# Thirty contraction rows for every score and maxima product of an attention kernel, with the tiles cleared for it and three exponentials one step later

## The chip, the cores and the metric

The kernel runs on one core of one Trainium2 chip. The metric is the device time of one execution in microseconds (us). The engines are named as the profile names them: PE (TensorE, with PEld for its weight loads), DVE (VectorE), ACT (ScalarE), POOL (GpSimd) and SP (SyncE, which here issues most of the DMAs).

## The reference

Two attentions over the same 2048 x 448 input are computed in float32 and mixed by a gate for each row. A is local: each position looks at eight positions, two apart, behind it. B is full attention with 16 heads of 28 columns.

```python
g = _sigmoid((x * gate_w).sum(-1, keepdims=True))
a = _A_ref(x, A_wqkv, A_wo)     # sliding window of 8, dilation 2, 16 heads of 28
b = _B_ref(x, B_wqkv, B_wo)     # scores = q k^T / sqrt(28), softmax, times v, times wo
return g * a + (1 - g) * b
```

## The kernel before

Every float32 operand of a projection or of the scores is held as a rounded value ("hi") and the rest ("lo"); a product is then three products, hi x hi, hi x lo and lo x hi, summed in PSUM. The order of the instructions on each engine is written out by hand (the framework only adds the waits), so an engine does its work in the order in which the program emits it.

**First stage.** The inputs are loaded and split, and q, k, v of both attentions are projected. `init_kh` writes 1.0 over a whole key tile `KH` (128 x 2048) on POOL: a head's 28 rows are later loaded over it, and the rows above keep the ones. The very first split is a cast on DVE (L443), which gives the first 512 columns of `xh`, the first operand of the first projection. Between the projections PE computes the first maxima products, on half the array (64 rows).

**Main stage.** Units are u = 0 to 15 (four heads by 512 queries each), and each has 16 steps, kt = 0 to 15, over blocks of 128 keys. In one step PE issues, in an order given by the list `WITH`: twelve score products (four heads a = 0 to 3, three terms each: token "a0" is KH x QH, "a1" is KH x QL, "a2" is KL x QH), up to three maxima products `s0` to `s2` (a later unit's queries `QP` times `KH`), and then the product `av` of the step before. Each head has a row group of 32 rows of the array, and products of different row groups run side by side. The term "a0" contracts 30 rows, the 28 of the head and two more, in which `QH` holds the negative maximum of the query (hi and lo) and `KH` holds ones; the other products contract 28 rows. ACT takes the exponential of two heads at a time (`P`, 128 x 1024). DVE reduces the maxima (`s1_max`, L155): first `s0` alone, then `s1` and `s2` in one reduction of 1024 columns. A PSUM tile that DVE or ACT still reads can't be written again, so PE's weight loads wait for them.

**Beside it.** The local attention A runs in eight chunks on POOL, DVE and ACT. A planner (`issue`) takes items from a list per engine, each with a key, a cost and the items it needs; an item that is late moves what needs it. ACT's items are the eight local exponentials (`a_softmax(c, 4)`, L679), issued behind the two exponentials of a step. ACT also copies the sums `osb` of the unit that has ended (`fin_copy`, L905, at the start of step kt = 1) and rounds `onhi`, the scaled output of that unit, 14 steps later (`fin_hi`, L943, at the start of kt = 15; the first unit's in two halves, at the start of kt = 0 and kt = 2 of the third unit).

**The end.** When the units are through, the output projection runs on PE alone (L886).

Of the kernel before, what the change touches and what calls it, by code (L numbers as in the profile page):

```python
# [16 lines left out]
NB, NJ, NG = 4, 16, 4  # L17
W, DIL = 8, 2
HALO = (W - 1) * DIL
SCALE = DH ** -0.5  # L20
NU = NG * NB
NMX = 192
# [3 lines left out]
def gated_mix_kernel(ctx: ExitStack, tc: tile.TileContext, xT, xn, gw, wA, wB, woAB, out):  # L26
# [48 lines left out]

    QP = [[cp.tile([128, 512], F32R, name=f"QP{i}{k}") for k in range(2)] for i in range(2)]

    def init_kh(t):
        nc.gpsimd.memset(t.bitcast(F32), 1.0)

    def pair(name):
        return pp.tile([128, 2, 512], F32, tag="P", name=name)
# [18 lines left out]
            r = D + 112 * g + DH * h  # L105
            dma_r(t[32 * h:32 * h + DH, c], src[r:r + DH, c])

    def load_part(u, name, src):
        g, b = divmod(u, NB)
        t = sp.tile([128, 512], F32R, name=name)  # L110
        for h in range(4):
            r = 112 * g + DH * h
            dma_r(t[32 * h:32 * h + DH, :], src[r:r + DH, 512 * b:512 * b + 512])
        return t
# [1 line left out]
    Qs = {}  # L116

    def load_q(u, low=True):
        Qs[u] = load_part(u, "QH", qk_hi), load_part(u, "QL", qk_lo)
        if low:  # L120
            load_nm(u)

# [18 lines left out]
    def s1_mm(n, bank, half=False):  # L141
        u, i = divmod(n, 64)
        qs, kc, h = i // 16, i // 4 % 4, i % 4
        if u == 0:
            qs, kc = i // 8 % 4, 2 * (i // 32) + i // 4 % 2
        if i == 0 and u + 1 < NU:
            load_qhi(u + 1)
        r = slice(64 * (h // 2), 64 * (h // 2) + 64) if half else slice(32 * h, 32 * h + DH)
        nc.tensor.matmul(bank, qhis[u][h % 2][r, 128 * qs:128 * qs + 128],  # L149
                         KH[u // NB % 3][r, 512 * kc:512 * kc + 512], start=True, stop=True)  # L150

# [54 lines left out]
            nc.sync.dma_start(nm[u].bitcast(F32)[:, 32 * a:32 * a + 32], r[32 * a:32 * a + 32, :])  # L206


    for t in KH:
        init_kh(t)  # L210
    t0 = pair("t0")[:, 0, :]
    nc.vector.memset(t0, 0.0)
    nc.vector.memset(zt, 0.0)
    nc.vector.memset(omt, 0.0)

    zero = nc.const_aps.tensor(0.0, [128, 512], F32).bitcast(F32R)

# [8 lines left out]
    if True:  # L226
# [259 lines left out]
        for n, t in enumerate(tiles[:-1]):  # L486
            wi = t[0]
            for w in loads:
                if loads[w] == n:
                    load_w(w)  # L490
            for w in splits:
                i, k = (n - splits[w][0]) * splits[w][1], splits[w][1]
                if 0 <= i < 4:
                    split_w(w, range(i, i + k))
            if n in (3, 5):
                split_x((n + 1) // 2)
            if n < FULL:
                project(n)
            else:
                project_halves(n, [S1_START <= m < S1_START + 80 for m in (n, n + 1)])  # L500
            if n == 0:
                split_x(1, (3,))
            if t[1] == "qk":
                for m in {0: (), 1: (0, 1)}.get(n, (n,)):
                    qk_tile(m, *tiles[m][2:4])
            elif t[1] == "v":
                add_halves(n, V[:, t[2], :, 0:DH])
            else:
                a_tile(n, t[2], t[3])
            if n == 1:  # L510
                split_x(1, range(3))
            if n == 4:
                for t in QP[1]:
                    nc.scalar.activation(t, t0, AF.Copy)
            while fini and fini[0][0] <= n:
                fini.pop(0)[1]()
            if n == 2:
                load_w(1, (False,))
            if n == 3:
                load_qhi(0)  # L520
            if n in (3, 8):
                load_k(0, KH[0], qk_hi, slice(0, 1024) if n == 3 else slice(1024, S))
            if n == 3:
                load_w(1, (True,))
            if n == 16:
                for i in (1, 2):
                    nc.sync.dma_start(a_scr[i][:, 0:NJ, :].rearrange("c j e -> c (j e)").rearrange(
                        "c (a b) -> c a b", b=NJ), omg[0:8, None, :].to_broadcast([8, 56, NJ]))
            if n == 32:
                nc.gpsimd.memset(V[:, :, :, DH:], 1.0)  # L530
            if n == 22:
                load_k(1, KH[1], qk_hi)
            if n == 62:
                load_k(0, KL[0], qk_lo)
            if parts and parts[0][0] <= n:
                _, u, t = parts.pop(0)
                max_store(u, max_turn(t))
            if finished and n < len(tiles) - 3:
                u = finished.pop(0)
                parts.append((n + 3, u, max_parts(u)))  # L540
            if n == 64:
                gate = []
                for sgn, dst in ((-1.0, g_t), (1.0, omg)):
                    e = sp.tile([128, NJ], F32, name="ez")
                    nc.scalar.activation(e, zt, AF.Exp, scale=sgn)
                    nc.gpsimd.tensor_tensor(out=e, in0=e, in1=V[:, 0, :, DH], op=ALU.add)
                    gate.append((dst, e))
            if n in (66, 68):
                nc.vector.reciprocal(*gate.pop(0))
            if n == 70:  # L550
                r = sp.tile([128, 32], F32, name="omr")
                nc.vector.transpose(r, omt)
                for a in range(4):
                    nc.sync.dma_start(og_scr.rearrange("(j p) -> j p", j=NJ)[:, 32 * a:32 * a + 32],
                                      r[32 * a:32 * a + NJ, :])
            if n == 76:
                load_q(0)
# [51 lines left out]
    def main_tiles():  # L609
        nonlocal mp, pm, maskt, actx, a1, a2, a3  # L610
        hctx.close()
        mp = ctx.enter_context(tc.tile_pool(name="mp", bufs=1))

        KH.append(mp.tile([128, S], F32R, name="KH2"))
        KL.append(mp.tile([128, S], F32R, name="KL1"))
        init_kh(KH[2])
        pm = ctx.enter_context(tc.tile_pool(name="pm", bufs=8))

        maskt = mp.tile([128, W, NJ, 2], F32, name="maskt")
        nc.gpsimd.memset(maskt, 0.0)  # L620
        for st, g, t, src in ((12, 2, KH[2], qk_hi), (30, 1, KL[1], qk_lo), (72, 2, KL[0], qk_lo),
                              (100, 3, KH[0], qk_hi), (136, 3, KL[1], qk_lo)):
            at("end", st, lambda g=g, t=t, src=src: load_k(g, t, src))
        for w in range(1, W):
            nc.gpsimd.memset(maskt[0:1, w, 0:DIL * w, :], -1e9 / SCALE)

        actx = ExitStack()
        a1 = actx.enter_context(tc.tile_pool(name="a1", bufs=1))
        a2 = actx.enter_context(tc.tile_pool(name="a2", bufs=2))
        a3 = actx.enter_context(tc.tile_pool(name="a3", bufs=5))  # L630
        for nme in ("k", "v"):
            for i in range(2):
                t = a1.tile([128, HALO + NJ, 56], F32, name=f"{nme}t{i}")
                kvt[nme, i] = t
# [384 lines left out]
    def scores(u, kt, cur):  # L1019
# [9 lines left out]
        for tok in WITH if k else ALONE:  # L1029
            if tok[0] == "s":  # L1030
                i = int(tok[1])
                if i < k:
                    s1_mm(n + i, bank[tok])
                if i == 0:
                    s1_max(n, 1, T1)
                elif i == 2 and k > 1:
                    s1_max(n + 1, k - 1, other[:, 0:k - 1, :])
                continue
            a, t = tok[0], int(tok[1])
            h = (int(a) + n) % 4  # L1040
            r = slice(32 * h, 32 * h + (DH + 2 if t == 0 else DH))
            nc.tensor.matmul(bank[a], (KH[g % 3], KH[g % 3], KL[g % 2])[t][r, ks], (qh, ql, qh)[t][r, :], start=(t == 0), stop=(t == 2))  # L1042
            if t == 2 and a in "20":
                if len(exps) < 5:
                    probs.append(pair("P"))
                p = probs[len(exps) % 5]
                e = nc.scalar.activation(p, one if a == "2" else mine, AF.Exp, scale=SCALE).ins  # L1047
                for o in exps[-5:-4]:
                    tc.declare_no_dep(e, o, query=mybir.DependencyQuery.ANY_SYNC,
                                      reason="PE has read what it wrote, and this one waits for PE")  # L1050
                for o in maxs[-4:]:
                    tc.declare_no_dep(e, o, reason="PE waited for it and the exponential waits for PE")
                exps.append(e)
                cur[(h + 3) % 4], cur[h] = p[:, 0, :], p[:, 1, :]
                yield len(cur)

    for u in range(NU):
        g, b = divmod(u, NB)
        for kt in range(NJ):
# [29 lines left out]
                at("dve", st + lag, lambda t=t, w=turned: w.update(r=counted(lambda: max_turn(t))))  # L1089
                at("end", st + lag, lambda v=v, w=turned: max_store(v, w["r"]))  # L1090
            issue("dve", st, DLIM)
            issue("act", st, 0)
            run("act", st)
            if prev is not None:
                do_av(prev)
# [46 lines left out]
```

## Time and profile before

| | |
|---|---|
| median of 3 runs | 896.78 us (896.74 to 896.83) |
| the profiled execution | 896.69 us, its span 894.9 us |
| PE, DVE, ACT, POOL busy | 99%, 83%, 72%, 71% of the span |
| granted TensorE clock | 1.00 in every stage |
| first and projection stage | about 0 to 248 us |
| main stage, 256 steps | about 248 to 820 us |
| output projection | about 820 us to the end |

The page of the profile counts an engine as busy while one of its instructions runs. Matmuls overlap, so PE's share says that it is never without work, not that it works at its peak. A row of a timeline gives the start, the duration (of the whole run of instructions, where a count "x2" follows), the engine, the line, the operation with the tiles it writes and reads, and in brackets how long the engine had been idle and what released it. For a matmul the form 30*128 means 30 rows of contraction and 128 columns of weights.

### The profile page before, as it was taken

To read this page: it belongs to the slowest core of one execution; us is meant where nothing else is said; L and a number is where in the kernel's file an instruction comes from. 1 tells how busy PE (TensorE), PEld (TensorE's weight loads), DVE (VectorE), ACT (ScalarE), POOL (GpSimd) and SP (SyncE) were. 2 spreads that over 40 slices of the span, in tenths; PEclk is the share of its full clock that TensorE was granted. 3 is DMA by queue.
4 is the path that set the end of the run, shared out by engine and by line. 5 is a ranking of instruction groups with operands and counts; after the bars stand their busy time and mean duration, and the time that the engine had idled before them with its cause. 6 is when DMAs were issued, how large, how long until landed. Compare 5 with 4: busy or idle time off the path is not lost.

```text
span 894.9 us, 20516 instructions
## 1 busy us (share of the span) xinstructions
PE 890.2 (99%) x8312; PEld 533.4 (60%) x8312; DVE 740.5 (83%) x962; ACT 642.4 (72%) x766; POOL 638.7 (71%) x505
## 2 busy tenths in 40 slices
PE   9999999999999999999999999999999999999998
PEld 7889999999954444444444444444444444434997
DVE  6688999999979999999999999999999999832220
ACT  7456434343378898898988989989888898897220
POOL 1499846464459789998999989999999799701000
PEclk9999999999999999999999999999999999999999
DMA  8886403454372241225225222533121322437781
GB/s 267 277 267 186 151 12 84 135 142 121 103 248 66 89 139 46 67 61 156 71 56 143 86 62 86 128 96 98 45 64 32 89 43 49 104 78 214 192 265 52
DMA packets 114038, 104.51 MB, mean 117 GB/s; under 512 B 75240, under 2 KB 82280, under 8 KB 113160
## 3 DMA queue, kind: packets, MB, share of 16 engines
q1 hardware_dynamic: 113512, 102.42, 40.7%
q8 instruction: 65, 1.06, 0.5%
q10 hardware_dynamic: 432, 0.79, 0.3%
q14 instruction: 29, 0.24, 0.1%
HBM read 62.20 MB, written 40.96 MB: 115 GB/s over the span
## 4 chain that ended last, share of the span: by engine, by line
PE 99%; ACT 0%; issue 0%; ACTq 0%
PE T L1042 31%; PE av L1008 28%; PE r L325 15%; PE r L320 8%; PE T L886 8%; PE r L149 4%; PE T L149 4%; PE r L220 0%; PE av L472 0%; ACT P L1047 0%; ACT res L895 0%; ACT onhi L943 0%; ACT L L679 0%; ACTq L943 0%
## 5 line engine op out<-in xcount | busy, mean ns | idle before, releaser
L1047 ACT ACTIVATE P<-T 128x1024 f32<-128x1024 f32 x512 | 496.8, 1023 | 59.6 <-PE T L1042 57.9
L155 DVE TENSOR_REDUCE MX<-T 128x1 f32<-128x512 f32 x470 | 442.5, 954 | 31.7 <-PE T L149 13.7
L1008 PE MATMUL av<-P,V 128*32 128x512 f32 x2048 | 272.7, 605 | 0.0
L1042 PEld LDWEIGHTS T<-QH,KH 30*128 30x128 f32 x1024 | 92.2, 181 | 229.1 <-ACT P L1047 196.5
L149 PE MATMUL T<-KH,QP 28*128 28x512 f32 x704 | 220.3, 456 | 0.1
L1042 PE MATMUL T<-QH,KH 30*128 30x512 f32 x1024 | 211.7, 489 | 0.2 <-ACT P L1047 0.2
L171 DVE TENSOR_REDUCE MX<-r 128x2 f32<-128x1024 f32 x160 | 192.9, 1221 | 20.1 <-PE r L149 16.3
L1042 PE MATMUL T<-QH,KL 28*128 28x512 f32 x1024 | 185.7, 393 | 0.0
L1042 PE MATMUL T<-QL,KH 28*128 28x512 f32 x1024 | 184.3, 392 | 0.0
L653 POOL TENSOR_TENSOR prod<-qt,kt 128x896 f32<-128x896 f32 x64 | 135.4, 2116 | 6.4 <-DMA kt<-a_scr 6.4
L397 ACT ACTIVATE raw<-r 128x896 f32<-128x896 f32 (+1 forms) x62 | 57.1, 921 | 94.5 <-PE r L325 91.9
L149 PE MATMUL r<-KH,QP 64*128 64x512 f32 x320 | 114.5, 391 | 0.0
L714 POOL TENSOR_TENSOR oat<-oat,prod 128x896 f32<-128x896 f32 x48 | 101.2, 2109 | 2.0
L149 PEld LDWEIGHTS T<-KH,QP 28*128 28x128 f32 x704 | 86.1, 181 | 26.7 <-ACT P L1047 17.7
L325 PE MATMUL r<-wh,xh 64*128 64x448 f32 (+1 forms) x504 | 99.6, 363 | 0.0
L709 POOL TENSOR_TENSOR prod<-vt,L 128x896 f32<-128x896 f32 x56 | 95.3, 1702 | 0.3
L398 POOL TENSOR_TENSOR ast<-raw 128x448 f32<-128x448 f32 x47 | 54.3, 1154 | 56.4 <-ACT raw L397 43.9
L1042 PEld LDWEIGHTS T<-QL,KH 28*128 28x128 f32 x1024 | 94.3, 185 | 0.0
L1042 PEld LDWEIGHTS T<-QH,KL 28*128 28x128 f32 x1024 | 93.3, 183 | 0.2
L1008 PEld LDWEIGHTS av<-P,V 128*32 128x32 f32 x2048 | 40.3, 107 | 77.9 <-issue 65.4
L325 PE MATMUL r<-wl,xh 64*128 64x448 f32 (+1 forms) x441 | 79.0, 365 | 0.0
L325 PEld LDWEIGHTS r<-wh,xh 64*128 64x128 f32 x504 | 77.9, 185 | 0.1
(122 smaller groups left out, 1138.8 us busy)
## 6 DMA issues: line engine op xcount, KB each, us to landing
a_scr<-ast SPq DMA_DIRECT2D x24, 448.0 KB
qk_hi<-qkh SPq DMA_DIRECT2D x24, 256.0 KB
qk_lo<-qkh SPq DMA_DIRECT2D x24, 256.0 KB
rbc<-rs SPq DMA_DIRECT2D x64, 64.0 KB
QP<-qk_hi SPq DMA_DIRECT2D x64, 56.0 KB
KL<-qk_lo SPq DMA_DIRECT2D x16, 224.0 KB
QH<-qk_hi SPq DMA_DIRECT2D x64, 56.0 KB
QL<-qk_lo SPq DMA_DIRECT2D x64, 56.0 KB
```

Source lines behind the costliest of these rows:

```text
L149: nc.tensor.matmul(bank, qhis[u][h % 2][r, 128 * qs:128 * qs + 128], KH[u // NB % 3][r, 512 * kc:512 * kc + 512], start=True, stop=True)
L155: i = nc.vector.tensor_reduce(MX[:, n % NMX:n % NMX + k], bank, axis=X, op=ALU.max)
L171: nc.vector.tensor_reduce(m, PM[k], axis=X, op=ALU.max)
L320: nc.tensor.matmul(bank, ws[c][rows, k, t[4]:t[4] + 128], x, start=first, stop=last)
L325: nc.tensor.matmul(bank[:, 0:cols], x, ws[c][rows, k, 0:cols], start=first, stop=last)
L653: nc.gpsimd.tensor_tensor(out=p, in0=qt[c], in1=kvt["k", c % 2][:, HALO - DIL * w:HALO - DIL * w + NJ, :], op=ALU.mult)
L709: nc.gpsimd.tensor_tensor(out=dst.rearrange("p j (h d) -> p j h d", d=DH), in0=kvt["v", c % 2][:, HALO - DIL * w:HALO - DIL * w + NJ, :].r ...
L714: nc.gpsimd.tensor_tensor(out=ows[c % 2][:, :, 0:56] if w == W - 1 else oat[c], in0=oat[c], in1=oat[c, w], op=ALU.add)
L886: writes(bank, nc.tensor.matmul(bank[:, :D], src, wo[c][k], start=(first and k == ks[0] and i == 0), stop=(last and k == ks[-1] and i == 2)))
L1008: nc.tensor.matmul(av[32 * h:32 * h + 32, :], V[:, kt, 4 * g + h, :], tiles_[h], start=(kt == 0), stop=(kt == NJ - 1), skip_group_check=True)
L1042: nc.tensor.matmul(bank[a], (KH[g % 3], KH[g % 3], KL[g % 2])[t][r, ks], (qh, ql, qh)[t][r, :], start=(t == 0), stop=(t == 2))
L1047: e = nc.scalar.activation(p, one if a == "2" else mine, AF.Exp, scale=SCALE).ins
```

## The change

Every score term and every maxima product of the main stage now contracts 30 rows (`ROWS = DH + 2`). So that the two added rows add nothing, `KL` and `QL` are cleared to zero once: `QL` becomes two fixed tiles, cleared on DVE at the start, and `KL` is cleared by a new POOL memset, `init_kl`. The memset of `KH[1]` is emitted later in the program text, beside that of `KL[0]`; that of `KL[1]` stands behind that of `KH[2]`, where the main stage's tiles are made. In `QP` the added rows already hold zeros. The third edit keeps the planner from issuing a local exponential in steps kt = 14 and kt = 0.

```diff
+ROWS = DH + 2
...
+    QL = [cp.tile([128, 512], F32R, name=f"QL{i}") for i in range(2)]
...
+    def init_kl(t):
+        nc.gpsimd.memset(t.bitcast(F32), 0.0)
...
-        Qs[u] = load_part(u, "QH", qk_hi), load_part(u, "QL", qk_lo)
+        Qs[u] = load_part(u, sp.tile([128, 512], F32R, name="QH"), qk_hi), load_part(u, QL[u % 2], qk_lo)
...
-        r = slice(64 * (h // 2), 64 * (h // 2) + 64) if half else slice(32 * h, 32 * h + DH)
+        r = slice(64 * (h // 2), 64 * (h // 2) + 64) if half else slice(32 * h, 32 * h + ROWS)
...
-    for t in KH:
-        init_kh(t)
+    init_kh(KH[0])
...
+    for t in QL:
+        nc.vector.memset(t.bitcast(F32), 0.0)
...
             if n == 4:
                 for t in QP[1]:
                     nc.scalar.activation(t, t0, AF.Copy)
+                init_kh(KH[1])
+                init_kl(KL[0])
...
         init_kh(KH[2])
+        init_kl(KL[1])
...
-            r = slice(32 * h, 32 * h + (DH + 2 if t == 0 else DH))
+            r = slice(32 * h, 32 * h + ROWS)
...
-            issue("act", st, 0)
+            if kt not in (NJ - 2, 0):
+                issue("act", st, 0)
```

**POOL at the start.** What stands on POOL behind the building of the identity matrix, with its waits; before:

```order
masks.py:199 AFFINE_SELECT ident<-ident 128x128 [waits Pool_49]
L83 MEMSET KH_151 128x2048
L83 MEMSET KH_152 128x2048
L235 TENSOR_TENSOR wl_425<-raw,wh_424 128x384 [waits DMAHW7_49,DMAHW0_49,Activation_49]
L235 TENSOR_TENSOR wl_425<-raw,wh_424 128x384 [waits Activation_49] x2
```

and now:

```order
masks.py:199 AFFINE_SELECT ident<-ident 128x128 [waits Pool_49]
L85 MEMSET KH_151 128x2048
L85 MEMSET KH_152 128x2048
L88 MEMSET KL_153 128x2048
L240 TENSOR_TENSOR wl_430<-raw,wh_429 128x384 [waits DMAHW7_49,DMAHW0_49,Activation_49]
L240 TENSOR_TENSOR wl_430<-raw,wh_429 128x384 [waits Activation_49] x2
```

The memset of `KH[1]` (KH_152) stands where it stood, since POOL has nothing else to do ahead of it, and no wait holds it back; the memset of `KL[0]` (KL_153) follows it directly.

**DVE at the start**, where the first cast waits for its input from DRAM; before:

```order
L212 MEMSET t_161 128x512
L213 MEMSET zt 128x16
L214 MEMSET omt 128x32
L443 CAST xh_181<-V 128x512
L448 TENSOR_TENSOR xl_185<-V,xh_181 128x512
```

and now:

```order
L215 MEMSET t_162 128x512
L216 MEMSET zt 128x16
L217 MEMSET omt 128x32
L219 MEMSET QL_155 128x512
L219 MEMSET QL_156 128x512
L448 CAST xh_184<-V 128x512
```

The two memsets of `QL` stand ahead of the cast.

**ACT around the end of the seventh unit** (two `P` rows are a step; `L` is the local exponential, `onhi` the rounding at kt = 15, `osb` the copy at the next unit's kt = 1); before:

```order
L1047 ACTIVATE P<-T_3241 128x1024
L1047 ACTIVATE P<-T_3237 128x1024
L679 ACTIVATE L<-L 128x256
L943 ACTIVATE onhi<-on 128x512
L1047 ACTIVATE P<-T_3241 128x1024
L1047 ACTIVATE P<-T_3233 128x1024
L1047 ACTIVATE P<-T_3241 128x1024
L1047 ACTIVATE P<-T_3237 128x1024
L905 ACTIVATE osb<-av 128x512
```

and now:

```order
L1055 ACTIVATE P<-T_3245 128x1024
L1055 ACTIVATE P<-T_3241 128x1024
L951 ACTIVATE onhi<-on 128x512
L1055 ACTIVATE P<-T_3245 128x1024
L1055 ACTIVATE P<-T_3237 128x1024
L687 ACTIVATE L<-L 128x256
L1055 ACTIVATE P<-T_3245 128x1024
L1055 ACTIVATE P<-T_3241 128x1024
L913 ACTIVATE osb<-av 128x512
```

The local exponential has moved behind the next step's two exponentials. Three of the eight move so, by one step each: this one, the one at the end of the second unit, which comes to stand directly ahead of the first half of `onhi`, and the one after that, whose chunk has become a step later. With them, items of three chunks on DVE, POOL and SP that need them stand up to a step later. PE's order is unchanged, instruction by instruction.

More of the change, by code (lines that the diff above doesn't have):

```diff
@@ L106, in load_k, with load_part @@
             dma_r(t[32 * h:32 * h + DH, c], src[r:r + DH, c])
-    def load_part(u, name, src):
+    def load_part(u, t, src):
         g, b = divmod(u, NB)
-        t = sp.tile([128, 512], F32R, name=name)
         for h in range(4):
```

## The prediction

> **What bounds the kernel now.** I read the page first: busy shares, then the chain that ended last.
>
> ```profile
> PE 890.2 (99%) x8312; PEld 533.4 (60%) x8312; DVE 740.5 (83%) x962; ACT 642.4 (72%) x766; POOL 638.7 (71%) x505
> PE 99%; ACT 0%; issue 0%; ACTq 0%
> ```
>
> PE is the chain from the first matmul to the last. So whatever delays PE's start is paid in full, and in the main stage a stall shows only as a product that starts later than its row group was free. The second view is the busy time of the main stage.
>
> ```profile
> 255.00:780.00 525.00, 524.82 (x5366) 218.79 (x5365) 494.31 (x698) 467.51 (x523) 479.43 (x334) 1.00 0.33 88
> ```
>
> DVE (third, 494.31) works 94% of these 525 us, ACT (fourth, 467.51) 89%: a gain on PE here can't exceed DVE's idle 30.7 us. The third view is the timeline of one step, about 2.2 us long.
>
> ```profile
> 390.83 1.23 DVE L155 TENSOR_REDUCE MX<-T 128x2 f32<-128x1024 f32 x1
> 391.93 0.18 PEld L1042 LDWEIGHTS T<-QH,KH 30*128 30x128 f32 x2 [0.84 <-ACT P L1047]
> 391.94 0.50 PE L1042 MATMUL T<-QH,KH 30*128 30x512 f32 x2
> 391.94 0.50 PE L149 MATMUL T<-KH,QP 28*128 28x512 f32 x1
> 392.04 0.19 PEld L1042 LDWEIGHTS T<-QL,KH 28*128 28x128 f32 x2
> 392.12 0.18 PEld L1042 LDWEIGHTS T<-QH,KH 30*128 30x128 f32 x2
> 392.12 0.49 PE L1042 MATMUL T<-QH,KH 30*128 30x512 f32 x1
> 392.28 0.40 PE L1042 MATMUL T<-QL,KH 28*128 28x512 f32 x2
> 392.28 0.39 PE L1042 MATMUL T<-QH,KH 30*128 30x512 f32 x1
> ```
>
> The step opens at 391.93. The weights of the second pair of 30-row terms load at 392.12, which is 0.06 after DVE's two-bank reduction ended (390.83 + 1.23 = 392.06). DVE's reduction, not PE, releases them.
>
> **Thirty rows for all products.** Here is what the different row counts cost now, by the groups of instructions.
>
> ```profile
> L1042 PE MATMUL T<-QH,KH 30*128 30x512 f32 x1024 | 211.7, 489 | 0.2 <-ACT P L1047 0.2
> L1042 PE MATMUL T<-QL,KH 28*128 28x512 f32 x1024 | 184.3, 392 | 0.0
> L149 PE MATMUL r<-KH,QP 64*128 64x512 f32 x320 | 114.5, 391 | 0.0
> ```
>
> The 30-row products look 97 ns dearer than the 28-row ones (489 against 392 ns). It isn't the rows: 64 rows take 391. In the step above the 28-row maxima product at 391.94, which also opens its row group, takes 0.50 like the 30-row ones beside it, and the 30-row product at 392.28, whose weights had been loaded ahead, takes 0.39. The 0.1 us is a weight load that nothing covers, and it stays.
>
> Nor does a change of the row count cost anything here. From 30 to 28: the 28-row weights at 392.04 load while the 30-row products of the same row groups run, 0.11 after the first load. From 28 to 30 in one row group: the product at 392.28 follows the maxima product of 391.94 after 0.34, no more than a 28-row product takes behind a 30-row one (391.94 to 392.28, also 0.34). So I take 0 for this part. Its bounds: a gain of the whole apparent 0.1 us on PE's chain in each of some 235 steps (704 maxima products, three to a step), 23 us, which is a rival below; and on the other side 1 ns a product (391 against 392 ns for 64 and 28 rows), under 1 us in all. The DMAs into `QL` and `KL` keep their sizes and their places ahead of their users.
>
> **The memsets at the start.** Each row that decides here:
>
> ```profile
> 1.25 3.54 POOL L83 MEMSET KH<- 128x2048 f32 x2
> 0.91 0.48 DVE L212 MEMSET t<- 128x512 f32 x1 [0.91 <-PEq L1134]
> 1.35 0.07 DVE L213 MEMSET zt<- 128x16 f32 x1
> 4.64 0.43 DVE L443 CAST xh<-V 128x512 fp32r<-128x512 f32 x1 [3.18 <-DMA V<-in_xT]
> 0.77 4.37 PE L220 MATMUL r<-const-float32-0.0 128*128 128x512 f32 x10 [0.77 <-PEq L1134]
> 5.22 0.71 PE L320 MATMUL r<-xh,wh 128*128 128x512 f32 x2
> 6.89 0.63 PE L320 MATMUL r<-xh,wh 128*128 128x512 f32 x2
> 7.36 0.62 PE L320 MATMUL r<-xl,wh 128*128 128x512 f32 x2
> ```
>
> The two `QL` memsets cost DVE 2 x 0.48 = 0.96 us from about 1.5 on, and DVE is idle until 4.64: nothing. POOL's memsets don't hold DVE's back (the one at 1.35 took 0.07 with POOL's first memset running); if they did, the 0.96 would come on top of the wait weighed next.
>
> POOL's order hasn't set its tiles out of DVE's way. Two memsets of 1.80 us each fill 1.25 to 4.79, and the third, of `KL[0]`, now follows at 4.73 (they overlap by 0.06) and ends at 6.53. The cast comes at 4.64, the only DVE instruction of this kind near it. What can happen to such a cast shows elsewhere.
>
> ```profile
> 783.15 1.29 POOL L947 TENSOR_TENSOR onlo<-on,onhi 128x512 fp32r<-128x512 f32 x1 [2.49 <-DVE KH L830]
> 783.29 1.40 DVE L829 CAST KH<-wor 128x448 fp32r<-128x448 f32 x1
> 785.62 0.35 DVE L829 CAST KH<-wor 128x448 fp32r<-128x448 f32 x1
> 817.08 1.29 POOL L947 TENSOR_TENSOR onlo<-on,onhi 128x512 fp32r<-128x512 f32 x1 [8.11 <-DVE onhi L941]
> 817.92 0.73 DVE L862 CAST onhi<-oar 64x512 fp32r<-64x512 f32 x1 [0.92 <-DMA oar<-oa_scr]
> 809.76 0.43 DVE L862 CAST oahi<-oar 128x512 fp32r<-128x512 f32 x1 [7.40 <-DMA oar<-oa_scr]
> ```
>
> A cast that starts under a POOL instruction waits for it: 1.40 and 0.73 instead of 0.35 and 0.43, each ending 0.25 to 0.28 behind POOL. The cast of the start took its plain 0.43, as at 809.76, though the second memset covered its first 0.15; either a memset doesn't hold a cast, or the wait fell into the cast's own start. So the bounds are 0 and a wait for the whole third memset, to 6.53 + 0.28 = 6.81 instead of 5.07: 1.74 us. As the first projection (5.22) needs the cast and PE has no slack from 6.89 on (two matmuls each 0.47), all of it would be paid. I take 0: the cast starts 0.09 ahead of the third memset. But a DMA that lands 0.1 us later turns this round.
>
> [...]
>
> **`KL[1]`.** This memset of 1.80 us stands behind that of `KH[2]` on POOL.
>
> ```profile
> 254.95 0.21 POOL L192 TENSOR_TENSOR nmt<-nmv,nmt 128x16 fp32r<-128x16 f32 x1
> 261.60 2.13 POOL L653 TENSOR_TENSOR prod<-qt,kt 128x896 f32<-128x896 f32 x1 [6.44 <-DMA kt<-a_scr]
> 259.25 0.20 DVE L201 STREAM_TRANSPOSE nms<-nmt 128x32 f32<-128x32 f32 x1
> ```
>
> It moves `nmt` to 256.75; DVE wants it at 259.25, and POOL waits for a DMA until 261.60 anyway. Nothing; without that cover it would be 1.8 us.
>
> **The exponentials.** Three move one step on. The dear place is the end of the seventh unit, beside the same place of the fifth.
>
> ```profile
> 498.75 1.94 ACT L1047 ACTIVATE P<-T 128x1024 f32<-128x1024 f32 x2 [0.29 <-PE T L1042]
> 500.57 0.42 ACT L679 ACTIVATE L<-L 128x256 f32<-128x256 f32 x1
> 500.88 0.63 ACT L943 ACTIVATE onhi<-on 128x512 fp32r<-128x512 f32 x1
> 505.83 1.02 ACT L1047 ACTIVATE P<-T 128x1024 f32<-128x1024 f32 x1
> 390.60 1.94 ACT L1047 ACTIVATE P<-T 128x1024 f32<-128x1024 f32 x2 [0.35 <-PE T L1042]
> 397.41 1.94 ACT L1047 ACTIVATE P<-T 128x1024 f32<-128x1024 f32 x2
> ```
>
> With `L` and `onhi` in one gap three steps took 498.75 to 505.83, 7.08; without `L` 390.60 to 397.41, 6.81. At most 0.27 comes back; as `L` still falls into these steps, I take 0.2. At the end of the second unit the move does the reverse: `L` (0.42) comes to stand beside a half of `onhi`, two thirds of the pile above, so I give 0.15 back. The third place stands free both times. The queues behind them: items of three chunks on DVE and POOL a step later (the same work), and on SP eight stores of a chunk behind four query loads for a later unit. For what such reordering does to a step I leave 0.5 either way. Sum: 0 - 0.2 + 0.15 + 0 = -0.05, and 896.69 - 0.05 is 896.6 for the execution profiled, which lies 0.09 below the median of 896.78; I say 896.7.
>
> **The rivals.**
>
> A, forecast: as summed, 896.7, its own range 896.2 to 897.3. Chance 0.45.
>
> B, the cast waits for the third memset: 896.7 + 1.74 = 898.4, give or take the 0.5: 897.9 to 899.0. For it the two long casts and POOL's memsets without a gap between them; against it the cast's plain 0.43 under a memset. Chance 0.27. A measurement of this kernel can tell about 0.2% from no change, so 898.57 is the line: 0.12 of the 0.27 lies beyond it.
>
> C, the row count does matter, and what reads as a bare weight load is a switch: up to 235 x 0.1 = 23 us less, 873; DVE's idle 30.7 us would allow it. The timeline of the step speaks against it. Chance 0.14, all faster.
>
> D, slower: B happens, and PE's clock falls back in the gap. PE's warm-up products ran 0.44 apart (4.37 / 10), a pair at 6.89 takes 0.47 to the next pair, so 0.235 each: PE started at about half rate. After B's gap, 5.14 to 6.96, it may start so again; 4.4 us at 0.44 do 10 products instead of 18.7, which loses 2.0 us: 900.4. It decides whether 1.8 us without matmuls suffice; no such gap is in the trace. Chance 0.14, with any other loss beyond 898.57 in it.
>
> [...]
>
> **How the numbers follow.** Faster: C, 0.14. Same: A and 0.15 of B, 0.60. Slower: 0.12 of B and D, 0.26. The range holds A and B and some of D: 895.6 to 899.8.
>
> **What would show it.** The start of the first cast and its end (5.07 or 6.81) and PE's first `xh` product (5.22 or 6.96) decide A, B and D. The groups of L1042 and L149 with their new 30 rows should keep their means: 489 or so for the term that opens a row group, 392 for the others, and the weight load 0.06 behind DVE's reduction; a mean that falls by tens of ns for the opening terms, or main-stage steps that shorten, would make C right. The three steps around 498.75 should take 6.9. I am wrong if the time lies outside the range, above all below it.

## The result

The changed kernel takes 898.73 us (median of 13 runs, 897.14 to 900.66) against 896.83 us before (13 runs, 896.49 to 897.53): ratio 1.002, interval 1.0013 to 1.0027. It is slower by 1.9 us, where no change was forecast.

The 13 runs don't agree as those of before do, and the profile lists the mean granted TensorE clock of each: five show 1.000 and lie between 897.14 and 898.64, eight show 0.997 to 0.999 and lie between 898.73 and 900.66. (A stretch of 3.4 us at half the clock, as found below, lowers this mean to 0.998; 0.999 also stands beside runs of ordinary length, as in the first kernel below.) The execution whose trace follows is the fastest, 897.14 us with a span of 895.3 us. So this trace holds the part of the loss that every run has; the rest had to be found in another kernel's trace.

From the page after, busy times and the start of the chain, as shown of before:

```profile
PE 889.3 (99%) x8312; PEld 533.0 (60%) x8312; DVE 742.4 (83%) x964; ACT 642.5 (72%) x766; POOL 642.4 (72%) x507
PE 99%; DMA 0%; DVE 0%; ACT 0%; issue 0%
```

PE is still the chain, but DVE and a DMA have come into it. The timeline of the start, after, one engine behind the other:

```profile
1.25 3.55 POOL L85 MEMSET KH<- 128x2048 f32 x2
4.73 1.80 POOL L88 MEMSET KL<- 128x2048 f32 x1
1.51 1.03 DVE L219 MEMSET QL<- 128x512 f32 x2
4.50 2.32 DVE L448 CAST xh<-V 128x512 fp32r<-128x512 f32 x1 [1.96 <-DMA V<-in_xT]
6.85 0.69 DVE L453 TENSOR_TENSOR xl<-V,xh 128x512 fp32r<-128x512 f32 x1
0.77 4.60 PE L225 MATMUL r<-const-float32-0.0 128*128 128x512 f32 x10 [0.77 <-PEq L1143]
6.96 0.70 PE L325 MATMUL r<-xh,wh 128*128 128x512 f32 x2 [1.58 <-DVE xh L448]
```

The cast that took 0.43 us takes 2.32. It starts 0.23 ahead of the third memset and still ends 0.28 behind it (6.82 against 6.53), and PE's first projection starts at 6.96 instead of 5.22, after 1.58 us without a matmul. That is rival B to 0.01 us.

The groups of the main stage, after, and its busy times:

```profile
L1050 PE MATMUL T<-QH,KH 30*128 30x512 f32 x1024 | 212.0, 489 | 0.0
L1050 PE MATMUL T<-QL,KH 30*128 30x512 f32 x1024 | 183.4, 388 | 0.0
L1050 PE MATMUL T<-QH,KL 30*128 30x512 f32 x1024 | 186.0, 393 | 0.0
L153 PE MATMUL T<-KH,QP 30*128 30x512 f32 x704 | 220.7, 458 | 0.1
255.00:780.00 525.00, 525.00 (x5370) 218.61 (x5362) 494.96 (x699) 468.30 (x524) 482.75 (x344) 1.00 0.33 88
```

The two groups of before that stand neither above nor in the prediction:

```profile
L149 PE MATMUL T<-KH,QP 28*128 28x512 f32 x704 | 220.3, 456 | 0.1
L1042 PE MATMUL T<-QH,KL 28*128 28x512 f32 x1024 | 185.7, 393 | 0.0
```

The opening term keeps its 489 ns, as forecast. One mean has moved by more than 2 ns: the `QL` product went from 392 to 388 ns. (The maxima's mean lies anywhere between 455 and 458 in the traces of this document, with 28 rows and with 30.)

PE issues the same 8,302 matmuls in the same order behind the warm-up products in both kernels. So the n-th of one trace can be set against the n-th of the other. The table gives how much later (+) each kernel's product starts than that of before (us), at the first projection and at six times of before; the experiments' rows are used below.

```
                              first    30    250    500    520    700    end
after                         +1.74  +1.30  +1.31  +0.97  +0.70  +0.52  +0.43
KL[0] cleared on DVE           0.00  +0.20  +0.64  +0.39  +0.10  -0.01  -0.11
after, 17 warm-ups            +1.74  +1.29  +1.31  +1.61  +1.31  +1.13  +1.06
before, memset added          +1.74  +2.85  +2.84  +2.78  +2.78  +2.78  +2.77
rows alone                     0.00  -0.30  -0.30  -0.72  -0.71  -1.03  -1.13
exponentials alone             0.00  -0.16  -0.16  -0.12  -0.39  -0.18  -0.15
start laid out anew           +0.11  -0.28  +0.16  -0.34  -0.32  -0.68  -0.69
memset in slices              +2.03  +1.59  +1.59  +1.60  +1.60  +1.63  +1.62
memset added, 17 warm-ups     +2.36  +1.65  +1.65  +1.58  +1.62  +1.64  +1.67
maxima rows alone              0.00  -0.08  -0.08  -0.18  -0.18  -0.16  -0.21
score rows alone              +0.15  +0.19  +0.20  -0.27  -0.23  -0.54  -0.59
28 rows for all               +0.03  +0.72  +0.72  +0.42  +0.42  +0.23  +0.17
```

Of the 1.74 us after keeps 1.30 from 30 us on. Of the 0.44 between them, 0.40 is not the wait being made up. It arises between 13 and 17 us, where four products of before start up to 0.11 late each, and all twelve kernels gain 0.37 to 0.41 on before there, those that start on time too (rows alone from +0.10 to -0.30). So it is a delay in before's own execution, for a split, it seems: DVE's splits there start at 13.83 us, against 13.03 to 13.53 in three kernels that start on time. A single execution has such places; two more are `KL[0]` cleared on DVE and the start laid out anew, which both lose 0.44 between 30 and 250 us. From 250 us to the end 0.88 us comes back. The rest, +0.43, is the difference of the two profiled executions (897.14 - 896.69 = 0.45). Three things had to be settled: the memset, the eight longer runs, and the 0.88.

### The profile page after: what moved, and what is told of

It is laid out like the page before. It is cut to its first block, busy times and chain, and to the rows that moved or that the text cites. A ratio compares the mean times of both kernels' runs of the same rounds, so it can differ in the third digit from the quotient of the medians.

```text
span 895.3 us, 20523 instructions
## 1 busy us (share of the span) xinstructions
PE 889.3 (99%) x8312; PEld 533.0 (60%) x8312; DVE 742.4 (83%) x964; ACT 642.5 (72%) x766; POOL 642.4 (72%) x507
## 4 chain that ended last, share of the span: by engine, by line
PE 99%; DMA 0%; DVE 0%; ACT 0%; issue 0%
PE T L1050 31%; PE av L1016 29%; PE r L330 15%; PE r L325 8%; PE T L894 8%; PE T L153 4%; PE r L153 4%; DMA V<-in_xT 0%; PE av L477 0%; DVE xh L448 0%; ACT res L903 0%
## 5 line engine op out<-in xcount | busy, mean ns | idle before, releaser
L153 PE MATMUL T<-KH,QP 30*128 30x512 f32 x704 | 220.7, 458 | 0.1
L1050 PE MATMUL T<-QH,KL 30*128 30x512 f32 x1024 | 186.0, 393 | 0.0
L1050 PE MATMUL T<-QL,KH 30*128 30x512 f32 x1024 | 183.4, 388 | 0.0
L153 PEld LDWEIGHTS T<-KH,QP 30*128 30x128 f32 x704 | 86.0, 181 | 26.0 <-ACT P L1055 15.9
L1050 PEld LDWEIGHTS T<-QL,KH 30*128 30x128 f32 x1024 | 93.8, 184 | 0.0
L1050 PEld LDWEIGHTS T<-QH,KL 30*128 30x128 f32 x1024 | 92.9, 182 | 0.2
```

## The experiments

**Which edit is late at the start.** The first kernel takes the third memset off POOL and clears `KL[0]` on DVE, which is idle there; nothing else differs from after.

```diff
-    for t in QL:
+    for t in (*QL, KL[0]):
         nc.vector.memset(t.bitcast(F32), 0.0)
...
                 init_kh(KH[1])
-                init_kl(KL[0])
```

> The changed kernel with KL[0] cleared on DVE behind the two QL tiles (DVE idle until about 4.5 us) and no third memset on POOL. Theory (the third memset holds the first cast, and PE's clock suffers from the gap): the cast ends near 5.07 and PE's first projection starts near 5.22, mean clock 1.000 in every run, median 895.6 to 896.1, spread under 1 us: the profile after was 0.88 us shorter than that before in the main stage. Rival (the loss is the main stage's: the thirty rows lower the clock or the moved exponentials cost): the median stays near 898 or above, and mean clocks of 0.997 to 0.999 remain.

Measured: 896.61 us (11 runs, 895.86 to 897.37) against 896.73 before, ratio 0.9997, interval 0.9988 to 1.0005. The whole loss is gone, and with it the lower clocks: none of the 11 runs shows under 0.999. The median is 0.5 above the 895.6 to 896.1 expected. DVE's timeline at the cast:

```profile
2.92 1.76 DVE L219 MEMSET KL<- 128x2048 f32 x1 [0.38 <-issue]
4.60 0.47 DVE L448 CAST xh<-V 128x512 fp32r<-128x512 f32 x1
```

The cast starts 0.04 earlier than in before and takes 0.04 longer: it ends at 5.07 in both, 0.28 behind the end of `KH[1]`'s memset. In before's trace and in those of the first nine kernels of the table the cast ends, to 0.01 us, at the later of two times: 0.43 behind its own start, or 0.28 behind the end of POOL's run of memsets.

The reverse adds that memset to before, and nothing else.

```diff
     for t in KH:
         init_kh(t)
+    nc.gpsimd.memset(KL[0].bitcast(F32), 0.0)
```

> The kernel before with nothing but the third memset (KL[0], 1.8 us) behind the two of KH on POOL at the start; 28 rows and the old exponentials. Theory: the first projection starts near 6.96, the median rises by 1.3 us from the start and by more where the clock falls, to 898 to 900, with a spread of some us and mean clocks below 1. Rival (the loss comes from the rows or the exponentials): the median stays within 1.4 us of 896.8 and every clock is 1.000.

Measured: 899.47 us (9 runs, 896.43 to 899.70), ratio 1.0023, interval 1.0014 to 1.0032. Seven runs lie at 899.25 to 899.70, two at 896.43 and 896.63. Here the profiled execution is one of the long ones (899.47, mean clock 0.998). Its timeline of the start, POOL, DVE and PE:

```profile
1.25 3.54 POOL L83 MEMSET KH<- 128x2048 f32 x2
4.74 1.80 POOL L211 MEMSET KL<- 128x2048 f32 x1
4.79 2.03 DVE L444 CAST xh<-V 128x512 fp32r<-128x512 f32 x1 [3.33 <-DMA V<-in_xT]
0.77 4.09 PE L221 MATMUL r<-const-float32-0.0 128*128 128x512 f32 x10 [0.77 <-PEq L1135]
6.96 0.70 PE L321 MATMUL r<-xh,wh 128*128 128x512 f32 x2 [2.10 <-DVE xh L444]
8.62 1.05 PE L321 MATMUL r<-xh,wl 128*128 128x512 f32 x2
9.47 1.05 PE L321 MATMUL r<-xh,wh 128*128 128x512 f32 x2
11.58 0.63 PE L321 MATMUL r<-xh,wh 128*128 128x512 f32 x2
```

And the window 7.60 to 11.00 us, first of this kernel (the number before the last two is the granted clock):

```profile
7.60:11.00 3.40, 3.40 (x9) 2.72 (x9) 3.05 (x7) 2.55 (x7) 0.00 (x0) 0.50 0.64 157
```

then of after:

```profile
7.60:11.00 3.40, 3.40 (x16) 2.78 (x16) 3.34 (x8) 1.91 (x6) 0.00 (x0) 1.00 0.80 218
```

This is the second part of the loss. The first projection is 1.74 late here too; 0.66 us after it the clock falls and is granted at 0.50 for 3.4 us, and PE does 9 products where after, at 1.00, does 16. The 7 missing products at 0.23 us each are 1.6 us, and in the table this kernel is 2.85 behind at 30 us where after is 1.30: 1.55 more. That is rival D, seen in its own row. Why not in after, whose PE has a gap too? Here PE had sped up ahead of its gap: the last four warm-up products take 1.40 us from 3.47 on, against 1.91 from 3.46 in after. After's trace records the clock at 1.00 from 5.80 on, so of its gap of 1.58 us, which began earlier, only 1.16 lie behind the rise, where all 2.10 do here. In the kernel with slices below the gap is 1.87 us, and its ten warm-up products take 4.61, as slow as after's 4.60, so that at most 1.87 lie behind the rise. Neither falls. That the gap behind the rise decides is the author's estimate from these three traces, not tested.

**Is it the gap that lowers the clock?** Two kernels fill PE's gap with warm-up products, after and the kernel just shown, and change nothing else.

```diff
-    warm(10)
+    warm(17)
```

After with seventeen:

> The changed kernel with 17 warm-up products on PE instead of 10, so that PE works through most of the gap in which the cast waits. Theory: the cast still ends near 6.81 and the first projection starts near 6.96, but the clock is 1.000 in every run and the spread of 3.5 us goes: median about 897.2, that of the changed kernel's undisturbed executions. Rival (the clock falls for another reason, in the main stage): times still spread from 897 to 900.7 and the median stays near 898.7. If the extra products run at half rate throughout, they end near 8.1 and delay the start by some 1.2 us more.

Measured: 898.02 us (12 runs, 897.15 to 900.80), ratio 1.0017, interval 1.0008 to 1.0025. The expectation did not come true in full: the median is 0.8 above 897.2, and two long runs are left, 899.67 and 900.80, the latter with a clock of 0.998. But ten of the 12 runs lie at 897.15 to 898.18, where after has four of its 13 below 898.2. Its timeline of PE:

```profile
0.77 5.78 PE L225 MATMUL r<-const-float32-0.0 128*128 128x512 f32 x17 [0.77 <-PEq L1143]
6.96 0.71 PE L325 MATMUL r<-xh,wh 128*128 128x512 f32 x2 [0.41 <-DVE xh L448]
```

The gap is 0.41 us; the first projection, 6.96, waits for the cast as it does in after. In the table this execution loses 0.6 us once, between 410 and 430 us, where DVE waits 0.65 for a DMA (`fsum`); on both sides of that it draws ahead as after does.

Before with the memset and seventeen:

> The kernel before with the third memset in one piece and seventeen warm-up products instead of ten. Theory: the memset keeps the cast out as before (first projection at 6.96 us, +1.74, of which 1.3 to 1.4 is left from 30 us on), but PE has no gap over 0.5 us, the granted clock stays at 1.00 and the time is 896.73 + 1.35 = 898.1 us (897.9 to 898.4). Rival: the granted 0.50 from 7.6 to 11.0 us in the run with ten products has another cause than the gap, and the time stays at 899.5 us.

Measured: 897.93 us (11 runs, 897.76 to 898.38), ratio 1.0015, interval 1.0006 to 1.0024. The theory gave 898.1, the rival 899.5. Its timeline of PE:

```profile
0.77 6.97 PE L221 MATMUL r<-const-float32-0.0 128*128 128x512 f32 x17 [0.77 <-PEq L1135]
7.58 0.64 PE L321 MATMUL r<-xh,wh 128*128 128x512 f32 x2
```

There is no gap. Its pairs start 0.46 to 0.48 us apart from 7.58 to 9.91, as after's do at a clock of 1.00 from 8.16 on, where the pairs at 0.50 above take 0.85 and more; the mean clock of the execution is 1.000. With seven products more in a place where PE waits anyway, every run drops below 898.4, where seven of nine stood at 899.25 or more. So the gap is what lowers the clock in these runs; the late cast itself costs 1.2 us between the medians. More warm-up products are no mend, since they run past the first projection's place when most of them run at half rate: in the profiled execution the seventeen took 6.97 us, 0.41 each where a product of after's pairs takes 0.23, and held it to 7.58, +2.36 and not the +1.74 expected.

**What the cast waits for.** The same added memset, cut into eight.

```diff
-    nc.gpsimd.memset(KL[0].bitcast(F32), 0.0)
+    for c in range(0, S, 256):
+        nc.gpsimd.memset(KL[0][:, c:c + 256].bitcast(F32), 0.0)
```

> The kernel before with a memset of KL[0] behind KH's two as in the run with the memset alone, but cut into eight instructions of 256 columns each (0.22 us apiece). Theory: GpSimd instructions that follow each other without a gap keep the cast out until the last one ends, so the cast ends at about 6.8 us and the time is 899.5 us as with the memset in one piece. Rival: the cast waits only for the instruction in progress, ends by 5.4 us, and the time is 896.7 to 897.0 us.

Measured: 898.94 us (10 runs, 898.15 to 900.75), ratio 1.0026, interval 1.0017 to 1.0035. The timeline of POOL and DVE:

```profile
4.74 2.09 POOL L212 MEMSET KL<- 128x256 f32 x8
4.73 2.38 DVE L445 CAST xh<-V 128x512 fp32r<-128x512 f32 x1 [3.26 <-DMA V<-in_xT]
```

The cast ends at 7.11, 0.28 behind the last slice (6.83). From its recorded start on, eight boundaries between POOL instructions have gone by (one behind `KH[1]`'s memset and seven between slices), and it was let in at none. So what counts is not which of two instructions is recorded as started first, but where POOL's run of them ends; smaller pieces don't end it. How long a gap on POOL would have to be was not tested. Five runs lie at 898.15 to 898.34, as the late cast alone would give, and five at 899.55 to 900.75; the median falls between the two groups, off both times expected, and the end of the cast decides for the theory.

**The 0.88 us.** Rows alone: the first kernel of this section without the exponential rule.

```diff
-            if kt not in (NJ - 2, 0):
-                issue("act", st, 0)
+            issue("act", st, 0)
```

> Thirty rows alone: QL and KL[0] cleared on DVE at the start, KL[1] on POOL at the main stage, the exponentials where they were before. If the rows bring the slow drift of 0.88 us in the main stage, the median is 895.7 to 896.1 and equal to the run with the exponentials moved, within 0.2. If the drift comes from the exponentials, it is near 896.8. If a row switch cost 0.1 us a step, it would be near 875.

Measured: 896.03 us (11 runs, 895.43 to 896.61), ratio 0.9993, interval 0.9984 to 1.0001. In the table it draws ahead by 0.83 from 250 us to the end. It is not equal to the run with the exponentials moved (896.61), as had been expected; that difference is taken up below. The kernel before with the memset and the one with the memset and seventeen warm-ups, which keep 28 rows, stay within 0.07.

Which products? First the maxima alone, in before.

```diff
-        r = slice(64 * (h // 2), 64 * (h // 2) + 64) if half else slice(32 * h, 32 * h + DH)
+        r = slice(64 * (h // 2), 64 * (h // 2) + 64) if half else slice(32 * h, 32 * h + DH + 2)
```

> The kernel before with 30 rows for the 704 maxima products of the main stage alone; the second and third score products keep 28. In the runs with 30 rows for all of them PE's products draw ahead of those of before by 0.8 us between 300 and 850 us, and in the runs with 28 not at all. Theory 1 (a product that follows one of another row count in its row group pays a few ns, and a maxima product always runs between score products of 30 and 28 rows): this kernel still mixes 30 and 28, so it gains little, 0 to 0.3 us, 896.4 to 896.7 us. Theory 2 (the 704 maxima products are what gains, some 1.2 ns each or 3.7 ns a step): the whole 0.8 us, 895.9 us. With the prediction's own step (row counts cost nothing) it gains 0.

Measured: 896.67 us (11 runs), ratio 1.0001, interval 0.9992 to 1.0010; 0.13 in the table. Then the score products alone, which is the kernel with the rows alone and its maxima set back to 28:

```diff
-        r = slice(64 * (h // 2), 64 * (h // 2) + 64) if half else slice(32 * h, 32 * h + ROWS)
+        r = slice(64 * (h // 2), 64 * (h // 2) + 64) if half else slice(32 * h, 32 * h + DH)
```

> The kernel with all products at 30 rows, the early clears of KL[0] and QL on VectorE and no exponential rule (896.03 us), with the maxima products set back to 28 rows, so that the three score products have 30 rows and the maxima 28. Theory 1 (mixing costs): the score products no longer change among themselves, so a part of the gain stays, 0.4 to 0.8 us between 300 and 850 us: 896.0 to 896.4 us. Theory 2 (the maxima products are what gains): no gain, 896.7 us.

Measured: 895.89 us (11 runs, 895.42 to 896.44), ratio 0.9990, interval 0.9981 to 0.9999; 0.79 in the table. The score products carry the gain. Here the maxima, at 28 rows, stand between score products of 30, and that costs 0.04 at most (0.79 against 0.83). Last, 28 rows for every product, so that the `QL` product is what it was and only its predecessor changes.

```diff
-            r = slice(32 * h, 32 * h + (DH + 2 if t == 0 else DH))
+            r = slice(32 * h, 32 * h + DH)
```

> The kernel before with 28 rows for the first score product too, which leaves out the two rows by which it takes the maxima off, so its output is not the reference's; all its products of the main stage now have 28 rows. In the runs with 30 rows for the score products only the QL product, the one that follows the QH product in its row group, got shorter (392 to 389 ns), the KL product behind it did not (393 to 394). Theory 1 (the step from 30 to 28 rows between two products of one row group costs about 3.4 ns): the QL product takes 389 ns here too, and PE draws ahead by 0.6 to 0.9 us between 300 and 850 us: 895.9 us. Theory 2 (a QL product of 30 rows is itself the shorter): the QL product keeps 392 ns and nothing is gained, 896.7 us.

Measured: 896.17 us (11 runs, 895.99 to 897.03), ratio 0.9994, interval 0.9985 to 1.0004. The groups of instructions on its page, with 28 rows throughout:

```profile
L1042 PE MATMUL T<-QH,KH 28*128 28x512 f32 x1024 | 211.4, 488 | 0.1
L1042 PE MATMUL T<-QL,KH 28*128 28x512 f32 x1024 | 183.6, 389 | 0.0
L1042 PE MATMUL T<-QH,KL 28*128 28x512 f32 x1024 | 186.6, 394 | 0.0
```

and the same product in the kernel with the maxima rows alone, where it follows a 30-row product as before:

```profile
L1042 PE MATMUL T<-QL,KH 28*128 28x512 f32 x1024 | 183.9, 392 | 0.0
```

A `QL` product of 28 rows takes 392 ns behind one of 30 and 389 behind one of 28; of 30 rows behind 30 it takes 388. So it is the change from 30 rows to 28 between two score products of a row group that costs some 3 ns, not the count. A change at the other places shows no such price: the maxima above, and the opening term, 488 to 489 ns whatever stands ahead of it. Four row groups run side by side, so by estimate a step gains one such price: 256 steps by 3.3 ns are 0.84 us. With 28 rows throughout, the draw was 0.55, a little short of the 0.6 to 0.9 expected.

**The exponentials**, alone, in before (the two lines of the rule).

> The kernel before with the exponential rule alone. Theory: it gives back about 0.14 us at the end of the seventh unit (510 to 520 us) and takes about 0.1 us at the end of the second (300 to 340 us), as the matching of PE's products shows in the three kernels that have the rule; sum about 0, so 896.7 us (896.5 to 896.9), ratio 1.000. Rival: the 0.58 us between the medians of the two kernels with KL[0] cleared on VectorE (896.61 with the rule, 896.03 without) is the rule's price, and this kernel takes 897.3 us.

Measured: 897.01 us (11 runs, 896.55 to 898.17) against 896.71, ratio 1.0005, interval 0.9997 to 1.0014: just above the 896.5 to 896.9 of the theory, and below the rival's 897.3. ACT at the end of the seventh unit, in the timeline of after, which has the same rule:

```profile
499.71 1.94 ACT L1055 ACTIVATE P<-T 128x1024 f32<-128x1024 f32 x2 [0.36 <-PE T L1050]
501.54 0.63 ACT L951 ACTIVATE onhi<-on 128x512 fp32r<-128x512 f32 x1
502.06 1.94 ACT L1055 ACTIVATE P<-T 128x1024 f32<-128x1024 f32 x2
503.86 0.44 ACT L687 ACTIVATE L<-L 128x256 f32<-128x256 f32 x1
504.17 1.96 ACT L1055 ACTIVATE P<-T 128x1024 f32<-128x1024 f32 x2
506.49 1.96 ACT L1055 ACTIVATE P<-T 128x1024 f32<-128x1024 f32 x2
```

Three steps take 499.71 to 506.49, 6.78, against 7.08 before. All four kernels with the rule gain 0.27 to 0.30 in the table between 500 and 520 us, the others move by at most 0.04. In the kernel with the exponentials alone the whole main stage still comes out at 0: it loses 0.17 at the end of the second unit (from -0.16 at 250 us to +0.01 at 340) and 0.21 between 520 and 700. What stays open is whether the rule costs some tenths over many runs, as the medians would have it (897.01 against 896.71; 896.61 with it and 896.03 without). The interval of the first takes in 1, the second compares two kernels at 0.9997 and 0.9993 whose intervals overlap, and the traces show no such price.

**A start without any memset near the cast.**

```diff
-    for t in (*QL, KL[0]):
-        nc.vector.memset(t.bitcast(F32), 0.0)
+    nc.vector.memset(KH[1].bitcast(F32), 1.0)
...
-                init_kh(KH[1])
+                nc.scalar.activation(KL[0][0:1, 0:1], zt[0:1, 0:1], AF.Copy)
+                for t in (KL[0], *QL):
+                    init_kl(t)
```

> Thirty rows, no exponential rule, and the start laid out anew: KH[1] cleared on VectorE from 1.51 us, GpSimd holds KH[0]'s memset alone until 3.0, and KL[0] and the QL tiles follow on GpSimd behind a one-element ScalarE write that comes after the first projections. Theory: the first cast starts with its DMA at 4.50 us, takes 0.43 and ends at 4.93 instead of 5.07, PE's first projection starts at 5.08 instead of 5.22, and the time is 896.03 - 0.14 = 895.9 us (895.5 to 896.2). Rival: the end of the ten warm-up products at half rate (5.17 to 5.38 in the runs so far) takes the cast's place, the first projection stays at 5.22, and the time stays at 896.0 us.

Measured: 896.00 us (11 runs, 895.51 to 896.82), ratio 0.9992, interval 0.9983 to 1.0001: no gain over 896.03. The timeline of DVE and PE:

```profile
4.75 0.43 DVE L447 CAST xh<-V 128x512 fp32r<-128x512 f32 x1 [1.15 <-DMA V<-in_xT]
5.33 0.70 PE L324 MATMUL r<-xh,wh 128*128 128x512 f32 x2
```

Neither account of the start held, though the time lies in the theory's range. The cast did start with its DMA, but the DMA landed at 4.75 here, not 4.50; it comes anywhere between 4.50 and 4.79 in these traces, so `KH[1]`'s memset, over at 4.79, hides little.

The lowest median is that of the kernel with 30 rows for the score terms, 28 for the maxima, and the clears of `KL[0]` and `QL` on the idle DVE: 895.89 us, 0.1% below before, its interval just clear of 1. The two other kernels with 30-row score terms and no late cast, 896.03 and 896.00 us, can't be told apart from it.

## Why the prediction was wrong

**The step that failed** is the term of the memsets at the start: "I take 0: the cast starts 0.09 ahead of the third memset." It measured 1.74 at the first projection and 1.30 from 30 us on. The two bounds had been right, 0 and 1.74, and the choice between them was made by the recorded starts of the cast and the third memset. That the one recorded first goes first was the author's estimate; no row of before showed it. What this reading passed over is the second memset, which still ran when the cast came (until 4.79 against 4.64): the cast was waiting already, and the third memset followed without a gap. In all five traces with the third memset the cast ends behind POOL's last memset, in four of them although it is recorded as started 0.01 to 0.23 us ahead of the memset that kept it out. The row that should have warned was the prediction's own first one: two memsets in 3.54 us, one behind the other without a gap, and the cast's end 0.28 behind the second, within the 0.25 to 0.28 by which the two long casts ended behind POOL. Before's trace alone could not settle it, since 4.64 + 0.43 and 4.79 + 0.28 are both 5.07. Two later traces speak for the second: casts recorded from 4.60 us, behind a memset of DVE's own that ran until 4.68, end at 5.07 as well and take 0.47. So "the cast's plain 0.43 under a memset" was no evidence against the waiting.

**Rival B** was the mechanism, to 0.01 us at the cast and at the first projection. Its time, 898.4, compares with 897.93 in the kernel with 28 rows whose clock stays up, and with 897.14 in the fastest run of after, where the rows gave 0.88. It had 1.74 paid in full; against before 1.30 is seen, and 0.40 of the difference is the delay that before's own execution has at 13 to 17 us.

**Rival D** was right as well, for most runs: with 28 rows 2.77 us at the end of the trace, 899.47, against its 900.4. It had 2.0 us for the clock, lost from the end of the gap on; in fact the clock falls 0.66 us after PE has begun again, stands at 0.50 for 3.4 us, and 1.55 is lost. To D's question, whether 1.8 us without matmuls suffice, the traces answer for 2.10, which did, and for 1.58 and 1.87, which did not. The same program falls in some executions and not in others: seven of after's 13 have a mean clock of 0.997 or 0.998. B, D and the rows add up to the median: 896.83 + 1.30 + 1.55 - 0.88 = 898.8, where 898.73 was measured, just beyond the line of 898.57 that had divided no change from slower. A median of runs with D and runs without it falls on the side of the more frequent. The stated range, 895.6 to 899.8, holds it because it was drawn to take in B and some of D, not because of the sum.

**Rival C** had the right sign, not the size. The 0.1 us of the opening term is a weight load that nothing covers, as argued from the step at 391.93 (0.50 us for 28 rows that open a row group, 0.39 for 30 whose weights were loaded ahead): it is 488 to 489 ns with 30 rows throughout, with 28 throughout and mixed. But the price of the change from 30 rows to 28 is 3 ns and not the 0 that the prediction took from two intervals of 0.34 us, which a trace in steps of 0.01 us could not tell apart. The two group means, 392 for 28 rows behind 30 and 391 for 64 rows, could not either: the 64-row products are in another stage.

**The exponentials** came out as worked out at their two places: 0.2 was forecast at the end of the seventh unit and 0.27 to 0.30 measured, 0.15 back at the end of the second and 0.17 measured. Another 0.21 was given back later, within the 0.5 left for such reordering.

**The rest held**: `QL`'s memsets took 1.03 us of DVE's idle time and delayed nothing (the cast's start is put down to its DMA), and after is 1.31 behind at 250 us and 1.30 at 340, so `KL[1]`'s memset cost nothing.

**What stays open:** two of nine runs of before with the memset took 896.43 and 896.63 us, as if the cast had not waited. And not every long run is accounted for: five of after lie between 899.06 and 900.66, above the 898.8 of the sum, and some long runs show no lower mean clock (899.53 of before with the memset, 900.75 with slices, 899.67 of after with seventeen warm-ups). No trace of such a run was taken.

## What to carry to other kernels

When a DVE cast and POOL's memsets share a stretch, don't ask which starts first but where POOL's run of instructions ends: handed three clears or more in a row, POOL kept the cast out until the last in all five traces, and emitting a clear later in the program moves nothing if that engine has nothing else to do (`KH[1]`'s ended at 4.80 us in after, at 4.79 in before). Read the end of a suspect instruction against the end of the other engine's, not its duration; and where PE must wait near its start, count a gap of two microseconds as one that can cost the clock besides (2.10 us did, 1.58 and 1.87 did not in their traces). Put clears on an engine that is idle, and not in front of the only instruction that PE waits for.

## What the hardware showed beside it

- The cast was kept out across eight boundaries of back-to-back POOL memsets and ended only 0.28 us behind the last (7.11 against 6.83).
- After a gap of 2.10 us on PE, whose last four warm-up products had sped up (1.40 us against 1.91 in after), the clock stood at 0.50 from 7.6 to 11.0 us: 1.55 us lost, nearly as much as the wait itself.
- A score product of 28 rows takes some 3 ns longer behind one of 30 rows in its row group than behind one of 28 (392 against 389 ns); over 256 steps that is 0.8 us, by estimate.
